# GpSimd's low-part subtractions cut into pieces of at most 256 columns, and one weight-rounding step moved from VectorE to ScalarE

## The chip, the cores and the metric

One core of a Trainium2 chip runs the program. The metric is the device time of one execution in microseconds, the median of several runs. The engines are TensorE (PE in the profile, with PEld its weight loads), VectorE (DVE), ScalarE (ACT), GpSimd (POOL) and SyncE (SP), which issues the DMAs here.

## The reference

Two batches of 3008 x 256 values go through a two-dimensional Fourier transform whose real part is kept, then through two MLPs in sequence over all 6016 tokens.

```
X = np.fft.fft(x, axis=1); X = np.fft.fft(X, axis=2); y = X.real
h = y @ w_in;   r = np.maximum(h, 0.0);  y = (r * r) @ w_out        # 256 -> 2048 -> 256
h = y @ w_in2;  g = h / (1 + np.exp(-1.702 * h));  out = g @ w_out2  # 256 -> 2048 -> 256
```

The weights arrive as float64.

## The kernel before

Matmuls run on operands that are each split in two: a high part, which is the value rounded to the matmul's format by ScalarE (tiles gh, and the first half of w, w2i, eo, ya, yb, yc), and a low part, which is the value minus the high part (tile gl, and the second half of the others). Three products (high x high, high x low, low x high) stand for one. The helper `sub` (L74, L75 in the profile) makes every low part; its first argument says whether VectorE or GpSimd does it, and tables (`LOW`, `LOWE`, `VSTEPS`) choose.

The program has a start (Fourier transform of the first batch), a long first stage, and a second stage. The first stage is a loop of 128 steps over (token block, slice of 128 hidden units). In a step TensorE makes one slice of hidden values in PSUM (`front1`, tile psa, L429 to L431, two psa buffers), VectorE takes it out of PSUM in three operations (p L686, h L688, h L689), ScalarE applies Relu, Square and the rounding (L695, L696, L698; in some steps VectorE does the first two in one operation, L693), and GpSimd in most steps subtracts (gl L75). Four steps later TensorE multiplies gh and gl by the second weights into psb (`back`, L444). A step's `front1` can only start when VectorE has emptied the psa buffer of two steps before.

Beside the steps, jobs run in the background by a table of starts, rates and due steps (`PLAN`): the Fourier transform of the second batch (`fold`, L260 to L278, `even_k`, `odd_k`), and the conversion of the float64 weights (`widen` and `widen_in`, which begin with `narrow`). `narrow` turns the two 32-bit words of each float64 into a float32: absolute value of the high word (ScalarE, L157), clamp (VectorE, L158), shift and mask (VectorE, L159), scaling of the low word by 2^-29 (L163 on ScalarE or L165 on VectorE), then two or three VectorE operations that merge them (L166, L168). The order of instructions on each engine within the first stage is set by a scheduler; each engine then runs its own list in that order, waiting on semaphores. GpSimd's list in the first stage is mainly `sub` in 128 x 752 pieces (two halves of 376 columns), besides folds (L260), sums (L188, L221, L581, L591) and `sub` of weights (128 x 1024, 128 x 512 and 128 x 384).

The second stage (from about 525 us) is written in a fixed order by hand. There `sub` is on VectorE alone, and GpSimd only does sums (L581, L591).

## Time and profile before

| | |
|---|---|
| median of 3 runs | 1037.11 us (1035.15 to 1038.47) |
| the profiled execution | 1035.54 us, of which the span from first to last instruction is 1033.8 us |
| PE busy | 971.6 us (94%) |
| DVE busy | 817.1 us (79%) |
| ACT busy | 616.4 us (60%) |
| POOL busy | 351.4 us (34%) |
[...]

The busy shares are means over stages with different limits. A time in the profile counts from the first instruction; an instruction's duration runs from its start to its end as recorded, and so contains any time that it stood still after it had started. The idle time of an engine and what ended it stand in the chain of waits.

### The profile page before, as it was taken

The numbers are of one execution on the slowest core, as the hardware profiler recorded it, in microseconds if no ns is written. First come the engines' busy times: TensorE is split into PE (matmuls) and PEld (weight loads), VectorE is DVE, ScalarE is ACT, GpSimd is POOL, SyncE is SP. The second block draws the span as 40 slices with busy tenths as digits, with TensorE's granted clock in tenths as the row PEclk, the third lists the DMA queues.
The fourth block names the chain that finished last, engine by engine and source line by source line (L and its number), as shares of the span: only waits on it lengthen the run. The fifth ranks groups of instructions, "written<-read, shape, count | busy, mean of one in ns | idle before, by whom it ended". The sixth has DMA issues, their size and how long they took to land.

```text
span 1033.8 us, 14043 instructions
## 1 busy us (share of the span) xinstructions
PE 971.6 (94%) x5496; PEld 939.3 (91%) x5496; DVE 817.1 (79%) x1088; ACT 616.4 (60%) x764; POOL 351.4 (34%) x216
## 2 busy tenths in 40 slices
PE   4879997899989999999989999999999999999998
PEld 4569887899989889898989999999999999999997
DVE  7995889886777579777658888887988888888875
ACT  2667576775788578797754554554555445454443
POOL 2546464444567446786815210102020020200000
PEclk9999999999999999999999999999999999999999
DMA  7531112101132112101342101000100001000000
GB/s 289 204 127 61 71 71 82 71 31 53 42 129 96 72 55 99 71 31 60 120 132 93 60 31 31 30 31 5 57 1 31 30 26 35 1 31 1 30 1 30
DMA packets 22914, 65.22 MB, mean 63 GB/s; under 512 B 1856, under 2 KB 14272, under 8 KB 19648
## 3 DMA queue, kind: packets, MB, share of 16 engines
q1 hardware_dynamic: 22848, 64.32, 17.4%
q8 instruction: 43, 0.70, 0.3%
q14 instruction: 23, 0.19, 0.1%
HBM read 43.13 MB, written 21.19 MB: 62 GB/s over the span
## 4 chain that ended last, share of the span: by engine, by line
PE 47%; DVE 5%; ACT 4%; issue 1%; POOL 1%; DMA 0%; DVEq 0%; POOLq 0%; ACTq 0%
PE psb L753 24%; PE psa L737 22%; ACT h L696 1%; ACT h L695 1%; DVE gl L75 1%; PE psb L444 1%; ACT gh L698 1%; POOL gl L75 1%; DVE g L789 0%; DVE ue L168 0%; DVE h L689 0%; DMA ydram<-o 0%; DVE p L686 0%; POOL raw L581 0%; DVE h L688 0%
## 5 line engine op out<-in xcount | busy, mean ns | idle before, releaser
L75 POOL TENSOR_TENSOR gl<-h,gh 128x752 fp32r<-128x752 f32 (+1 forms) x113 | 216.0, 1920 | 166.6 <-ACT gh L698 142.1
L444 PE MATMUL psb<-gh,w 128*128 128x376 f32 (+1 forms) x1024 | 240.6, 340 | 4.4 <-ACT o L557 3.5
L753 PE MATMUL psb<-gh,w 128*128 128x376 f32 (+1 forms) x1024 | 237.7, 334 | 0.0
L444 PEld LDWEIGHTS psb<-gh,w 128*128 128x128 f32 x1024 | 185.6, 192 | 6.8 <-ACT o L557 4.7
L753 PEld LDWEIGHTS psb<-gh,w 128*128 128x128 f32 x1024 | 182.9, 188 | 0.0
L695 ACT ACTIVATE h<-h 128x752 f32<-128x752 f32 (+1 forms) x116 | 96.5, 833 | 81.7 <-DVE h L689 77.8
L444 PE MATMUL psb<-gl,w 128*128 128x376 f32 (+1 forms) x512 | 133.7, 341 | 3.2 <-POOL gl L75 2.8
L818 ACT ACTIVATE g<-c 128x1128 f32<-128x1128 f32 (+1 forms) x64 | 73.7, 1152 | 100.1 <-DVE c L816 100.1
L753 PE MATMUL psb<-gl,w 128*128 128x376 f32 (+1 forms) x512 | 129.9, 335 | 0.4 <-DVE gl L75 0.3
L686 DVE SCALAR_TENSOR_TENSOR p<-n,w1n_t,psa 128x376 f32<-128x376 f32 (+1 forms) x128 | 76.5, 601 | 59.7 <-PE psa L431 59.5
L698 ACT CAST gh<-h 128x752 fp32r<-128x752 f32 (+1 forms) x128 | 105.0, 822 | 21.5 <-DVE h L693 14.0
L75 DVE TENSOR_TENSOR gl<-g,gh 128x1504 fp32r<-128x1504 f32 (+1 forms) x64 | 112.2, 1753 | 1.6 <-ACT gh L798 1.6
L429 PE MATMUL psa<-eo,w 128*128 128x376 f32 (+1 forms) x256 | 89.9, 351 | 24.6 <-DVE h L689 19.9
L798 ACT CAST gh<-g 128x1504 fp32r<-128x1504 f32 (+1 forms) x64 | 93.1, 1454 | 32.2 <-DVE g L789 32.2
L591 POOL TENSOR_TENSOR ue<-raw 128x376 f32<-128x376 f32 (+1 forms) x16 | 19.6, 1243 | 271.0 <-DVE ya L75 270.8
L444 PEld LDWEIGHTS psb<-gl,w 128*128 128x128 f32 x512 | 94.6, 193 | 4.8 <-POOL gl L75 4.0
L696 ACT ACTIVATE h<-h 128x752 f32<-128x752 f32 (+1 forms) x116 | 96.6, 834 | 3.2
L753 PEld LDWEIGHTS psb<-gl,w 128*128 128x128 f32 x512 | 92.2, 188 | 1.0 <-DVE gl L75 1.0
L789 DVE TENSOR_TENSOR g<-g,c 128x1128 f32<-128x1128 f32 (+1 forms) x64 | 89.6, 1401 | 1.2 <-ACT g L818 1.2
L815 DVE TENSOR_TENSOR g<-g,psa 128x376 f32<-128x376 f32 (+1 forms) x64 | 35.0, 547 | 68.5 <-ACT g L814 68.5
L430 PE MATMUL psa<-eo,w 128*128 128x376 f32 (+1 forms) x256 | 86.4, 338 | 0.7 <-DVE eo L75 0.7
L431 PE MATMUL psa<-eo,w 128*128 128x376 f32 (+1 forms) x256 | 86.2, 337 | 0.0
(135 smaller groups left out, 1594.3 us busy)
## 6 DMA issues: line engine op xcount, KB each, us to landing
ydram<-o SPq DMA_DIRECT2D x18, 376.0 KB, 2.9
xt<-in_x SPq DMA_DIRECT2D x5, 1024.0 KB, 7.1
cst<-in_dfts SPq DMA_DIRECT2D x8, 570.0 KB, 5.5
raw<-ydram SPq DMA_DIRECT2D x6, 752.0 KB, 4.5
out<-o SPq DMA_DIRECT2D x11, 376.0 KB, 3.1
raw<-in_w1i SPq DMA_DIRECT2D x4, 1024.0 KB, 5.6
raw<-in_w1o SPq DMA_DIRECT2D x4, 1024.0 KB, 4.9
raw<-in_w2i SPq DMA_DIRECT2D x4, 1024.0 KB, 4.9
```

Of the source, the lines that this page charges most:

```text
L75: eng.tensor_tensor(out=o, in0=a, in1=f32(b), op=ALU.subtract)
L429: T.matmul(o, lhsT=w[:, 0, fs], rhs=t[:, par, 0, 0:wd], start=True, stop=False)
L430: T.matmul(o, lhsT=w[:, 0, fs], rhs=t[:, par, 1, 0:wd], start=False, stop=False)
L431: T.matmul(o, lhsT=w[:, 1, fs], rhs=t[:, par, 0, 0:wd], start=False, stop=True)
L444: T.matmul(acc[j][ec][:, s, 0:wd], lhsT=w[:, hl, e0:e0 + P], rhs=(gh, gl)[gi][:, s, 0:wd], start=(first and hl == 0 and gi == 0), stop=(la ...
L695: A.activation(out=hv, in_=hv, func=AF.Relu)
L696: A.activation(out=hv, in_=hv, func=AF.Square)
L698: last_a = A.copy(gh[:, :, 0:wd], hv)
L737: T.matmul(bank, lhsT=w[:, hl, slot * P:(slot + 1) * P], rhs=t[:, yl, i], start=(first and hl == 0 and yl == 0), stop=(hl == 1), skip_grou ...
L753: T.matmul(o[:, s, 0:wd], lhsT=w[:, hl, e0:e0 + P], rhs=g[:, 2 * i + s, 0:wd], start=(f == 0 and hl == 0 and g is gh), stop=(f == 15 and h ...
L789: V.tensor_tensor(out=g[:, 1:4, 0:pw], in0=g[:, 1:4, 0:pw], in1=c[:, :, 0:pw], op=ALU.mult)
L798: A.copy(gh[:, :, 0:pw], g[:, :, 0:pw])
```

## The change

Two things. `sub` on GpSimd is now issued in pieces: a new generator `pieces` walks over all dimensions but the first and the last and cuts the last into equal parts of at most 256 columns. VectorE's subtractions stay whole. And `narrow` always scales the low word on ScalarE: the set `RA`, which named the eight weight groups for which ScalarE did it, and the parameter `key` are gone.

```diff
-RA = {(0, 0, 0), (0, 0, 1), (0, 0, 2), (0, 0, 3), (0, 1, 1), (0, 1, 2), (0, 1, 3), (1, 0, 1)}
...
+    def pieces(*aps):
+
+        if len(aps[0].shape) > 2:
+            for i in range(aps[0].shape[1]):
+                yield from pieces(*(ap[:, i] for ap in aps))
+        else:
+            w = aps[0].shape[1]
+            k = -(-w // 256)
+            for i in range(k):
+                yield tuple(ap[:, i * w // k:(i + 1) * w // k] for ap in aps)
+
     def sub(eng, o, a, b):
-        eng.tensor_tensor(out=o, in0=a, in1=f32(b), op=ALU.subtract)
+        for o, a, b in pieces(o, a, b) if eng is G else ((o, a, b),):
+            eng.tensor_tensor(out=o, in0=a, in1=f32(b), op=ALU.subtract)
...
-    def narrow(raw, ue, key=None):
+    def narrow(raw, ue):
...
-        if key in RA:
-            yield lambda: A.activation(out=eu, in_=lw, func=AF.Copy, scale=2.0 ** -29)
-        else:
-            yield lambda: V.tensor_scalar(out=eu, in0=lw, scalar1=2.0 ** -29, scalar2=None, op0=ALU.mult)
+        yield lambda: A.activation(out=eu, in_=lw, func=AF.Copy, scale=2.0 ** -29)
```

On GpSimd's list, at the conversion of a pair of second-stage weight groups (tile w2i, with the low parts gl of the steps around it), before:

```order
L75 TENSOR_TENSOR gl<-h,gh 128x2x376 x3
L75 TENSOR_TENSOR w2i<-ue,w2i 128x512
L75 TENSOR_TENSOR w2i<-ue,w2i 128x384
L75 TENSOR_TENSOR gl<-h,gh 128x2x376
L75 TENSOR_TENSOR w2i<-ue,w2i 128x512
L75 TENSOR_TENSOR w2i<-ue,w2i 128x384
L75 TENSOR_TENSOR gl<-h,gh 128x2x376 x4
L75 TENSOR_TENSOR w<-ue,w 128x1024
```

The same place of the changed kernel (`sub` is now L86):

```order
L86 TENSOR_TENSOR gl<-h,gh 128x188 x12
L86 TENSOR_TENSOR w2i<-ue,w2i 128x128 x7
L86 TENSOR_TENSOR gl<-h,gh 128x188 x4
L86 TENSOR_TENSOR w2i<-ue,w2i 128x128 x7
L86 TENSOR_TENSOR gl<-h,gh 128x188 x16
L86 TENSOR_TENSOR w<-ue,w 128x256 x4
```

A gl is four instructions in place of one, a w four in place of one, and a half of w2i seven in place of two; their order among each other is the same here.

On VectorE's list, at the conversion of the last weight group of the first stage (tiles raw and ue; p and h belong to the steps), before:

```order
L165 TENSOR_SCALAR ue<-raw 128x1024
L158 TENSOR_SCALAR ue<-ue 128x1024
L686 SCALAR_TENSOR_TENSOR p<-n,w1n_t,psa 128x376
L159 TENSOR_SCALAR ue<-ue 128x1024
L688 TENSOR_TENSOR h<-p,psa 128x376
L689 TENSOR_TENSOR h<-p,psa 128x376
L166 SCALAR_TENSOR_TENSOR ue<-raw,ue 128x1024
```

The same place of the changed kernel (L169 was L158, L170 was L159, L174 was L166, L694 to L697 were L686 to L689):

```order
L169 TENSOR_SCALAR ue<-ue 128x1024
L694 SCALAR_TENSOR_TENSOR p<-n,w1n_t,psa 128x376
L170 TENSOR_SCALAR ue<-ue 128x1024
L696 TENSOR_TENSOR h<-p,psa 128x376
L697 TENSOR_TENSOR h<-p,psa 128x376
L174 SCALAR_TENSOR_TENSOR ue<-raw,ue 128x1024
```

Only the first row is gone; the rest keeps its order. On ScalarE's list at the same conversion, before (L157 is the absolute value, L695, L696 and L698 belong to the steps):

```order
L698 CAST gh<-h 128x2x376
L157 ACTIVATE ue<-raw 128x1024
L695 ACTIVATE h<-h 128x2x376
L696 ACTIVATE h<-h 128x2x376
L698 CAST gh<-h 128x2x376
```

And in the changed kernel (L168 was L157, L173 is the scaling of the low word, L703, L704 and L706 were L695, L696 and L698):

```order
L168 ACTIVATE ue<-raw 128x1024
L703 ACTIVATE h<-h 128x2x376
L704 ACTIVATE h<-h 128x2x376
L706 CAST gh<-h 128x2x376
L173 ACTIVATE ue<-raw 128x1024
```

The scaling now stands on ScalarE one step behind the absolute value. TensorE's list is the same in both kernels.

## Rows read from the trace of the kernel before

**Rows 1.** Busy time of each engine (instructions) in four stretches, us.
```profile
0.00:80.00 80.00, 55.09 (x290) 43.95 (x291) 68.64 (x102) 39.93 (x54) 33.43 (x25) 0.96 0.54 201
...
80.00:220.00 140.00, 125.56 (x692) 120.03 (x691) 114.13 (x163) 94.76 (x118) 75.34 (x40) 0.98 0.20 71
...
400.00:525.00 125.00, 113.87 (x638) 110.53 (x636) 89.94 (x133) 100.44 (x129) 92.26 (x58) 0.98 0.23 81
525.00:1034.00 509.00, 503.49 (x2902) 500.14 (x2901) 412.52 (x490) 252.65 (x301) 53.07 (x31) 1.00 0.09 32
```

**Rows 2.** Waits of TensorE's weight loads, 0 to 80 us: total, times, longest.
```profile
PEld psb L444 <- POOL gl L75: 2.0, 2, 1.8
```

**Rows 3.** The same view, 80 to 220 us.
```profile
PEld psa L429 <- DVE h L689: 13.7, 9, 2.5
```

**Rows 4.** The same view, 220 to 400 us.
```profile
PEld psa L429 <- DVE h L689: 5.4, 5, 3.5
```

**Rows 5.** The same view, 400 to 525 us.
```profile
PEld psa L429 <- DVE h L689: 6.1, 6, 2.1
...
PEld psb L444 <- POOL gl L75: 1.4, 1, 1.4
```

**Rows 6.** Timeline of POOL from 117 us: start, duration, instruction.
```profile
118.50 4.57 POOL L75 TENSOR_TENSOR gl<-h,gh 128x752 fp32r<-128x752 f32 x2 [6.93 <-DVE h L693]
```

**Rows 7.** Timeline of DVE from 117 us.
```profile
119.44 1.96 DVE L166 SCALAR_TENSOR_TENSOR ue<-raw,ue 128x1024 uint32<-128x1024 uint32 x1 [0.21 <-ACT ue L163]
121.33 0.60 DVE L686 SCALAR_TENSOR_TENSOR p<-n,w1n_t,psa 128x376 f32<-128x376 f32 x1
121.84 2.31 DVE L168 CUSTOM_DVE_ANT_0 ue<-ue 128x2048 uint16<-128x2048 uint16 x1
```

**Rows 8.** DVE by shape, 0 to 80 us: count, total us, mean ns, idle before.
```profile
L166 DVE SCALAR_TENSOR_TENSOR ue<-raw,ue 128x1024 uint32<-128x1024 uint32 x5 | 9.9, 1987 | 0.0
L158 DVE TENSOR_SCALAR ue<-ue 128x1024 f32<-128x1024 f32 x6 | 7.3, 1219 | 0.0
L168 DVE CUSTOM_DVE_ANT_0 ue<-ue 128x2048 uint16<-128x2048 uint16 x5 | 6.1, 1217 | 0.0
...
L271 DVE TENSOR_TENSOR xt<-xt 128x512 f32<-128x512 f32 x3 | 2.1, 690 | 0.1
...
L165 DVE TENSOR_SCALAR ue<-raw 128x1024 uint32<-128x1024 uint32 x1 | 0.7, 690 | 0.0
```

**Rows 9.** The same view, 80 to 220 us.
```profile
L276 DVE TENSOR_TENSOR xt<-xt 128x512 f32<-128x512 f32 x2 | 3.9, 1931 | 0.0
L158 DVE TENSOR_SCALAR ue<-ue 128x1024 f32<-128x1024 f32 x2 | 3.7, 1844 | 0.0
L265 DVE TENSOR_TENSOR xt<-t 128x512 f32<-128x512 f32 x2 | 3.5, 1746 | 0.0
```

**Rows 10.** The same view, 220 to 400 us.
```profile
L165 DVE TENSOR_SCALAR ue<-raw 128x1024 uint32<-128x1024 uint32 x5 | 8.0, 1605 | 0.0
L168 DVE CUSTOM_DVE_ANT_0 ue<-ue 128x2048 uint16<-128x2048 uint16 x4 | 7.2, 1798 | 0.0
```

**Rows 11.** The same view, 400 to 525 us.
```profile
L166 DVE SCALAR_TENSOR_TENSOR ue<-raw,ue 128x1024 uint32<-128x1024 uint32 x4 | 6.4, 1606 | 1.2 <-ACT ue L163 1.2
...
L165 DVE TENSOR_SCALAR ue<-raw 128x1024 uint32<-128x1024 uint32 x2 | 4.5, 2274 | 3.0 <-POOL w2i L75 3.0
```

**Rows 12.** Timeline of POOL from 276 us.
```profile
276.85 0.75 POOL L221 TENSOR_TENSOR ue<-ue 128x256 f32<-128x256 f32 x1 [1.23 <-DVE ue L168]
277.56 1.81 POOL L75 TENSOR_TENSOR gl<-h,gh 128x752 fp32r<-128x752 f32 x1
279.32 2.39 POOL L221 TENSOR_TENSOR ue<-ue 128x256 f32<-128x256 f32 x3
```

**Rows 13.** POOL by shape, 400 to 525 us.
```profile
L75 POOL TENSOR_TENSOR gl<-h,gh 128x752 fp32r<-128x752 f32 x35 | 66.2, 1903 | 30.0 <-ACT gh L698 19.0 <-issue 8.3 <-DVE p L686 1.6
```

**Rows 14.** ACT by shape, whole run.
```profile
L163 ACT ACTIVATE ue<-raw 128x1024 uint32<-128x1024 uint32 x8 | 9.1, 1142 | 0.0
```

## The prediction

> **What bounds the kernel now.** I read the busy times by stretch first, then who TensorE's weight loads wait for in each, then the durations of VectorE's and GpSimd's instructions by shape, and last the timelines at one wait. From 525 us on TensorE is busy 503.5 of 509 us [rows 1], and no instruction that the change touches runs there, since `sub` is on VectorE alone in that stage. Half of the time can therefore not move. Before that TensorE is busy 55 of 80 us, 125.6 of 140 us, and 113.9 of 125 us [rows 1]. What it waits for there is mostly one thing: `front1` waits for VectorE's h L689 to empty psa, 13.7 us from 80 to 220 us, 5.4 from 220 to 400, 6.1 from 400 to 525 [rows 3 to 5]. VectorE is busy 68.6 of the first 80 us and 114.1 of the next 140 [rows 1].

> Why is VectorE late? Its durations show it. The custom merge L168 takes 1.22 us in the first stretch and 1.80 on average from 220 to 400 us [rows 8, 10]; L158, which has the size of L165 (0.69 us when nothing is in its way), takes 1.22 and 1.84 [rows 8, 9]; L165 itself takes 1.61 and 2.27 later [rows 10, 11]. The timelines show what is in its way. At 118.50 us two gl of 128x752 start back to back on GpSimd and end at 123.07 [rows 6]. VectorE's L166 starts at 119.44 and needs 1.96 us; L168 starts at 121.84 and needs 2.31 us, to 124.15 [rows 7]. With 1.81 us for one gl [rows 12] the first ended near 120.3, and L166 ended 1.1 us later, which is about what it needs alone. So it stood still until the first gl was done, then ran; the second gl stood still meanwhile (the two need 3.6 us by 1.81 each and took 4.57), and L168 then waited until the second gl had ended. The two engines don't share whatever they contend for: one instruction has it to its end, and between two instructions that stand back to back on GpSimd the waiting VectorE instruction gets it. VectorE's L686, which reads PSUM, ran in 0.60 us in between, at 121.33, while the second gl still had most of its work to do [rows 6, 7]: it doesn't contend, and I take the same of L688 and L689, which read PSUM too.

> **Part 1: shorter GpSimd instructions, what VectorE gains.** A blocked VectorE instruction now waits for a piece in place of a whole gl. A gl took about 1.8 us, a piece will take some 0.57 (worked out below), so one meeting costs a third. Where several contending VectorE instructions follow one another, each meets a piece and the wait is not a third but up to the whole. Because the steps' L686, L688 and L689 stand between most of them and pieces pass beneath these, I take a third as left, two thirds as gained. The waits that I can see in the rows, mean less the time alone, times count:

> - 0 to 80 us: L166 5 x (1.99 - 1.2) = 3.9, L158 6 x (1.22 - 0.69) = 3.2 [rows 8]; 1.2 for L166 alone is from L168, which has the same length. Two thirds of 7.1 is 4.7.
> - 80 to 220 us: L276 2 x (1.93 - 0.69), L158 2 x (1.84 - 0.69), L265 2 x (1.75 - 0.69) [rows 9]; 0.69 for 512 columns of two inputs is L271's [rows 8]. That is 2.5 + 2.3 + 2.1 = 6.9. Two thirds is 4.6.
> - 220 to 400 us: L168 4 x (1.80 - 1.22) = 2.3 [rows 10]; two thirds is 1.5.
> - 400 to 525 us: L166 4 x (1.61 - 1.2) = 1.6 [rows 11]; two thirds is 1.1.

> **Part 2: the low words on ScalarE.** VectorE loses L165: 0.7 us in the first stretch, 8.0 in the third, 4.5 in the fourth [rows 8, 10, 11], durations that contain its waits. ScalarE gains eight instructions of 1.14 us [rows 14], 9.1 us. It is busy 100.4 of 125 us in the fourth stretch [rows 1], so they fit, but each delays a gh by up to 1.14 us. What is queued behind is a step's Relu, Square and rounding, and behind those gl and, four steps later, TensorE's `back`. With four steps in hand I count 1 us in all.

> **Part 3: what GpSimd pays.** From the start of the L221 at 276.85 to that of the gl is 0.71 us for 256 columns, and from the gl to the next L221 1.76 us for 752 [rows 12]. That is 2.1 ns a column and 0.16 us for each instruction, so a piece of 188 columns takes 0.16 + 0.40 = 0.56 to 0.57, four of them 2.25 and a gl 0.48 us more. From 400 to 525 us there are 35 gl [rows 13], 17 us more, where GpSimd is busy 92.3 of 125 us [rows 1]: 109, and the weights' pieces add some more. This is near full. The price is paid where TensorE waits for a gl: 2.0 us in two places of the first stretch and 1.4 us in one of the last [rows 2, 5]. In the last, gl stand in a queue, three of them make 1.4 us; the other two places make 1 us; for places that come to be such, where the end of gl and its use are close already, 1.5 us. Sum 4 us.

> [...]

> **The sum.** What VectorE gains reaches TensorE only where TensorE waits for it. Stretch by stretch: 0 to 80 us, 4.7 + 0.7 = 5.4 gained on VectorE, which is busy nearly throughout, but TensorE and ScalarE have their own turns in the start: I take 3. 80 to 220 us, 4.6 gained against 13.7 waited: 5, a little more than all of it, since other contending forms of that stretch are not in my list. 220 to 400 us, 8.0 + 1.5 against 5.4 waited: 4. 400 to 525 us, 4.5 + 1.1 against 6.1 waited: 4. That is 16, less 4 for GpSimd and 1 for ScalarE. So 11 us off the profiled execution of 1035.5 us gives 1024.5. The median of the runs, 1037.1, is 1.6 us above the profiled execution, so **1026 us**.

> Bounds: if all that TensorE waits behind VectorE goes, 13.7 + 5.4 + 6.1 and 5.4 in the start, and GpSimd costs nothing, 30.6 us go: 1006.5 for the median. If VectorE gains nothing from the pieces, see the second rival.

> **Rivals.** *More of it reaches TensorE*: the gain on VectorE exceeds what I counted, because forms that I left out wait as well and each wait delays all steps behind it. With 25 to 30 of the 30.6 us of the bound gone and 5 paid as above, 20 to 25 us: 1012 to 1017. For it: VectorE is freed of 9.5 and 5.6 us in the third and fourth stretch, about what TensorE waits there. Against: when VectorE is earlier, TensorE runs into ScalarE, which is busy 80% in the fourth stretch, or GpSimd.

> *The lock stays with GpSimd between pieces, and the kernel is slower.* If the pieces of one gl follow so closely that VectorE doesn't get in between, it waits for 2.25 us where it waited for 1.78. The waits counted above, 7.1 + 6.9 + 2.3 + 1.6 = 17.9, grow by 27%, 5 us; GpSimd's price of 4 doubles, as its gl are held by the same VectorE instructions and last longer; moving L165 alone gives back 4 to 8, the gain counted for the third and fourth stretch or half of it. With 1037.1 + 5 + 8 and less 4 to 8 the median is 1042 to 1046. It decides as soon as VectorE fails to get in at more than about half of the pieces' ends. Against it stands the wait shown above [rows 6, 7]: between two gl that stood back to back VectorE did get in. [...] No run here shows yet what happens between pieces that short.

> *GpSimd becomes the bound of the last stretch.* 109 us and the weights' pieces, and at each piece a chance to be held by VectorE for up to 1.2 us. If the fourth stretch takes 125 us as before or 3 us more, its gain of 4 is lost and up to 3 more: of the 11 us 4 to 7 remain, 1030 to 1033, and up to 1037 if the third stretch loses its 4 as well. For it: TensorE waits for a gl there already [rows 5]. Against: 16 us of room.

> **Chances.** My forecast (1018 to 1030) 0.50; more reaches TensorE (below 1018) 0.17; GpSimd bounds the fourth stretch (1030 to 1037) or the gain is hidden otherwise (to 1040) 0.20; the lock stays, or another loss (above 1040) 0.13. 0.3% is 3.1 us, about what can be told from no change here. Faster than 1034: 0.50 + 0.17 + half of the third, 0.76. Same 0.11, slower 0.13. The range that holds 8 in 10 is 1012 to 1038; the likeliest case alone has 1018 to 1030.

> **What would show it.** Step 1: L168 on VectorE near 1.3 to 1.4 us in every stretch, L158 and L159 near 0.8. If they stay at 1.5 and above, pieces don't let VectorE in. Step 2: no scaling of low words on VectorE, 17 on ScalarE (the small w1n included) and no new waits for gh. Step 3: pieces of 188 columns start 0.56 us apart when nothing interrupts; GpSimd's busy time in the fourth stretch rises by 17 us or more; TensorE's waits for gl, now 2.0 and 1.4 us, rise by 5 us at most. The second stage must begin some 11 us before 525 us and take as long as before; if it took longer, the whole argument would miss something. The prediction is wrong if TensorE's waits for h don't fall below 15 us in all, or if they do and waits for gl or ScalarE take their place.

## The result and the profile after

The changed kernel takes 1045.9 us, the median of 5 runs (1043.56 to 1047.14), against 1037.11 before: 1.0086 times, 95% interval 1.0075 to 1.0097. It is slower, by 8.8 us, where 11 us less were forecast. One of the runs of the kernel before that were made beside it took 5343 us, which doesn't move the median. The profiled execution took 1047.14 us, its span is 1045.4 us.

First the first view of before again, busy time of each engine by stretch (TensorE, its weight loads, VectorE, ScalarE, GpSimd, then granted TensorE clock as a share of full speed, DMA share, GB/s), now of after:

```profile
0.00:80.00 80.00, 56.23 (x286) 44.47 (x286) 63.59 (x98) 39.36 (x53) 40.56 (x50) 0.91 0.53 201
80.00:220.00 140.00, 128.09 (x725) 123.97 (x725) 113.38 (x171) 99.41 (x124) 107.98 (x149) 0.99 0.21 72
...
400.00:536.00 136.00, 114.87 (x629) 111.47 (x627) 86.72 (x126) 99.61 (x128) 114.75 (x190) 0.95 0.21 74
536.00:1045.00 509.00, 503.91 (x2903) 500.61 (x2902) 412.83 (x491) 253.12 (x301) 53.16 (x31) 1.00 0.09 32
```

The second stage begins at 536 us where it began at 525 [rows 1], and takes 509 us as before. All is decided in the first stage. From 80 to 220 us TensorE is busier than before (128.1 for 125.6 us); the last stretch takes 136 us for 125, and GpSimd is busy 114.8 us in it for 92.3. Over the whole run TensorE is busy 975.0 us for 971.6 and idle 70.4 for 62.2 (the spans less the busy times): of the 11.6 us by which the span grew, 8.2 are idle time, and 3.4 the same matmuls running longer. The granted clock goes with that: 0.91 for 0.96 in the first stretch and 0.95 for 0.98 in the last. The windows around two long waits of TensorE, same columns:

```profile
418.00:425.00 7.00, 0.89 (x6) 0.58 (x4) 1.00 (x2) 1.22 (x2) 7.00 (x16) 0.72 0.00 0
425.00:429.00 4.00, 3.37 (x11) 3.37 (x12) 4.00 (x6) 3.94 (x6) 1.82 (x4) 0.50 0.52 193
429.00:433.00 4.00, 4.00 (x19) 4.00 (x18) 3.33 (x5) 3.90 (x6) 3.74 (x5) 0.70 0.36 104
...
479.00:483.00 4.00, 3.56 (x12) 3.57 (x13) 3.90 (x7) 3.25 (x4) 0.00 (x0) 0.57 0.00 0
```

From 418 to 425 us TensorE was busy 0.89 of 7 us; from 425 to 429 the granted clock was 0.50, and behind the second wait, from 479 to 483 us, 0.57. Two weight loads took 0.64 us behind each wait (at 427.99 and 481.17 us), for 0.36 ahead of the first (at 416.16). So these two long waits were paid for twice.

Which waits, tells the view of what TensorE's weight loads wait for, the whole run of after: total, times, longest.

```profile
PEld psa L437 <- DVE h L697: 18.1, 9, 5.4
PEld psb L452 <- POOL gl L86: 15.0, 15, 2.0
PEld psb L452 <- ACT o L565: 9.3, 3, 7.0
```

Before, the same view had:

```profile
PEld psa L429 <- DVE h L689: 26.2, 22, 3.5
...
PEld psb L444 <- ACT o L557: 4.7, 4, 2.3
PEld psb L444 <- POOL gl L75: 4.0, 4, 1.8
```

So TensorE waits 8 us less for VectorE, 11 us more for GpSimd's gl, and 4.6 more for ScalarE's o (the store copy that empties psb). By stretch, from 80 to 220 us:

```profile
PEld psb L452 <- POOL gl L86: 5.5, 6, 2.0
PEld psa L437 <- DVE h L697: 5.3, 3, 1.8
```

The wait for h there fell from 13.7 us [rows 3] to 5.3, more than was forecast. From 400 to 540 us:

```profile
PEld psa L437 <- DVE h L697: 9.3, 4, 5.4
PEld psb L452 <- ACT o L565: 7.0, 1, 7.0
...
PEld psb L452 <- POOL gl L86: 3.6, 4, 1.5
```

Here the wait for h rose, from 6.1 us [rows 5] to 9.3, with one of 5.4 in it. The timelines show where that one comes from. VectorE, then TensorE's weight load that follows it:

```profile
471.44 5.92 DVE L169 TENSOR_SCALAR ue<-ue 128x1024 f32<-128x1024 f32 x1 [4.74 <-ACT ue L168]
477.27 0.59 DVE L694 SCALAR_TENSOR_TENSOR p<-n,w1n_t,psa 128x376 f32<-128x376 f32 x1
477.79 0.68 DVE L170 TENSOR_SCALAR ue<-ue 128x1024 uint32<-128x1024 uint32 x1
```

```profile
479.43 0.29 PEld L437 LDWEIGHTS psa<-eo,w 128*128 128x128 f32 x1 [5.43 <-DVE h L697]
```

And GpSimd, start, duration, instruction, number of instructions in the group:

```profile
455.48 6.67 POOL L86 TENSOR_TENSOR gl<-h,gh 128x188 fp32r<-128x188 f32 x12
462.10 2.98 POOL L86 TENSOR_TENSOR w2i<-ue,w2i 128x128 fp32r<-128x128 f32 x7
465.04 2.27 POOL L86 TENSOR_TENSOR gl<-h,gh 128x188 fp32r<-128x188 f32 x4
467.26 2.98 POOL L86 TENSOR_TENSOR w2i<-ue,w2i 128x128 fp32r<-128x128 f32 x7
470.18 6.62 POOL L86 TENSOR_TENSOR gl<-h,gh 128x188 fp32r<-128x188 f32 x12
```

L169 needs 0.68 us when nothing is in its way. It started at 471.44 and stood still until the last group of gl ended at 476.80: ten pieces ended while it waited, and only behind the last, where the row ended, did it get in. The step's L694, queued behind it on VectorE, came 5 us late, and with it the psa buffer for which TensorE then waited 5.43 us. At 512.21 us a second one, yb (128 x 378, 0.54 us alone), took 6.48 us (TensorE then waits 2.74); at 339.69 a third, L701, took 6.21, behind which TensorE had slack. Before, in the same place, the whole forms stood:

```profile
452.84 5.39 POOL L75 TENSOR_TENSOR gl<-h,gh 128x752 fp32r<-128x752 f32 x3
458.17 2.29 POOL L75 TENSOR_TENSOR w2i<-ue,w2i 128x512 fp32r<-128x512 f32 x2
460.40 1.83 POOL L75 TENSOR_TENSOR gl<-h,gh 128x752 fp32r<-128x752 f32 x1
462.18 2.28 POOL L75 TENSOR_TENSOR w2i<-ue,w2i 128x512 fp32r<-128x512 f32 x2
464.41 4.08 POOL L75 TENSOR_TENSOR gl<-h,gh 128x752 fp32r<-128x752 f32 x2
```

```profile
464.50 2.30 DVE L165 TENSOR_SCALAR ue<-raw 128x1024 uint32<-128x1024 uint32 x1 [0.48 <-POOL w2i L75]
```

There VectorE's L165 started at 464.50, took 2.30 us and was let in behind the first of the two gl, although GpSimd had worked without a pause for 12 us. In that row it arrived in the tenth instruction; in after's row L169 arrived in the 34th (both counts begin with one sum, L221 or L229, that runs without a pause ahead of the lines shown).

### The profile page after: what moved, and what is told of

Its sections match the earlier page's. It is cut to its first block, busy times and chain, and to the rows that moved or that the text cites. A ratio compares the mean times of both kernels' runs of the same rounds, so it can differ in the third digit from the quotient of the medians.

```text
span 1045.4 us, 14449 instructions
## 1 busy us (share of the span) xinstructions
PE 975.0 (93%) x5496; PEld 943.6 (90%) x5496; DVE 800.6 (77%) x1079; ACT 624.0 (60%) x773; POOL 446.6 (43%) x628
## 4 chain that ended last, share of the span: by engine, by line
PE 47%; DVE 4%; POOL 3%; ACT 2%; issue 1%; DMA 0%; DVEq 0%; POOLq 0%; ACTq 0%
PE psb L761 24%; PE psa L745 22%; POOL gl L86 2%; DVE ue L169 1%; PE psb L452 1%; DVE yb L86 1%; DVE gl L86 1%; ACT h L704 1%; ACT h L703 1%; POOL w2i L86 0%; DMA ydram<-o 0%; ACT gh L706 0%; POOL raw L589 0%; DVE h L697 0%; DVE h L696 0%
## 5 line engine op out<-in xcount | busy, mean ns | idle before, releaser
L86 POOL TENSOR_TENSOR gl<-h,gh 128x188 fp32r<-128x188 f32 (+1 forms) x452 | 296.9, 693 | 101.9 <-ACT gh L706 75.8
L452 PE MATMUL psb<-gl,w 128*128 128x376 f32 (+1 forms) x512 | 136.7, 344 | 10.7 <-POOL gl L86 10.7
L703 ACT ACTIVATE h<-h 128x752 f32<-128x752 f32 (+1 forms) x116 | 96.2, 832 | 67.1 <-DVE h L697 54.1
L694 DVE SCALAR_TENSOR_TENSOR p<-n,w1n_t,psa 128x376 f32<-128x376 f32 (+1 forms) x128 | 76.7, 601 | 70.1 <-PE psa L439 69.9
L761 PE MATMUL psb<-gl,w 128*128 128x376 f32 (+1 forms) x512 | 129.9, 335 | 0.4 <-DVE gl L86 0.3
L706 ACT CAST gh<-h 128x752 fp32r<-128x752 f32 (+1 forms) x128 | 104.9, 822 | 27.9 <-DVE h L701 24.6
L86 DVE TENSOR_TENSOR gl<-g,gh 128x1504 fp32r<-128x1504 f32 (+1 forms) x64 | 112.2, 1753 | 1.6 <-ACT gh L806 1.6
L704 ACT ACTIVATE h<-h 128x752 f32<-128x752 f32 (+1 forms) x116 | 96.3, 834 | 3.2
```

What stands on the lines that cost most here:

```text
L86: eng.tensor_tensor(out=o, in0=a, in1=f32(b), op=ALU.subtract)
L452: T.matmul(acc[j][ec][:, s, 0:wd], lhsT=w[:, hl, e0:e0 + P], rhs=(gh, gl)[gi][:, s, 0:wd], start=(first and hl == 0 and gi == 0), stop=(la ...
L703: A.activation(out=hv, in_=hv, func=AF.Relu)
L704: A.activation(out=hv, in_=hv, func=AF.Square)
L706: last_a = A.copy(gh[:, :, 0:wd], hv)
L761: T.matmul(o[:, s, 0:wd], lhsT=w[:, hl, e0:e0 + P], rhs=g[:, 2 * i + s, 0:wd], start=(f == 0 and hl == 0 and g is gh), stop=(f == 15 and h ...
```

## The experiments

A row is a run of GpSimd instructions with no idle time between them. Theory A: a long unbroken row of GpSimd instructions keeps a contending VectorE instruction out, and cutting makes rows long; beside that GpSimd is late by its own 0.45 us per gl. Theory B: the scaling moved to ScalarE does the harm. Theory C: only GpSimd's time counts, VectorE is not kept out. All times below are medians of 4 to 10 runs; the kernel before ran beside them with 1036.4 to 1036.8 us, and differences are against that, so that they can be added (the changed kernel: +8.8 against its 1037.1).

**The two parts alone.** In the first, the kernel before gets `pieces` and the new `sub`, nothing else. In the second, the changed kernel gets the old one back:

```diff
...
-        for o, a, b in pieces(o, a, b) if eng is G else ((o, a, b),):
-            eng.tensor_tensor(out=o, in0=a, in1=f32(b), op=ALU.subtract)
+        eng.tensor_tensor(out=o, in0=a, in1=f32(b), op=ALU.subtract)
```

> The kernel before with the pieces alone; the low words are scaled where they were (VectorE for eight groups). Theory A (a long unbroken row of pieces on GpSimd keeps a contending VectorE instruction out, and each gl takes 0.45 us longer): 1041 to 1048 us, and at least two VectorE instructions of 5 us or more that need 0.5 to 1.3 us alone. Theory B (the loss comes from the scaling that ScalarE took over, and the pieces gain): 1026 to 1032 us. Theory C (the pieces cost only GpSimd's 0.45 us per gl, VectorE is not kept out): 1038 to 1043 us with no VectorE instruction kept longer than 3 us.

> The changed kernel with whole subtractions on GpSimd: only the scaling of the low words is moved to ScalarE. A and C (the pieces do the harm): 1030 to 1036 us, since VectorE loses 13 us of work in the last two stretches and ScalarE has room. B (the moved scaling does the harm): 1042 to 1047 us, with a wait of TensorE for ScalarE's o near 425 us of 5 us or more, as in the changed kernel.

Pieces alone: 1045.4 us, +9.0, ratio 1.0078 (1.0051 to 1.0106). Scaling alone: 1031.9 us, -4.5, ratio 0.9961 (0.9948 to 0.9974). So the pieces do the harm, and B falls: the scaling on ScalarE is worth 4.5 us, and on top of it the pieces cost 13.3. With pieces alone TensorE also waits 6.7 us for o near 420 us, so that wait too is the pieces'. One detail of A's expectation missed: there is one VectorE instruction kept over 5 us (7.05 us at 469 us), not two.

**Where.** Only the gl of steps 16 to 75 cut, and the other half:

```diff
-    def sub(eng, o, a, b):
-        for o, a, b in pieces(o, a, b) if eng is G else ((o, a, b),):
+    def sub(eng, o, a, b, cut=False):
+        for o, a, b in pieces(o, a, b) if eng is G and cut else ((o, a, b),):
...
-            sub(G if i not in VSTEPS else V, gl[:, :, 0:pw], h[:, :, 0:pw], gh[:, :, 0:pw])
+            sub(G if i not in VSTEPS else V, gl[:, :, 0:pw], h[:, :, 0:pw], gh[:, :, 0:pw], 16 <= i < 76)
```

> The changed kernel, but only the gl of steps 16 to 75 are cut; the gl of the other steps and all weights are whole on GpSimd. By the shifts of the steps in the two traces the changed kernel gains 7.5 us between steps 15 and 45 and loses it before and behind. A: the gain stays and the later losses go, 1027 to 1033 us, no VectorE instruction kept longer than 3 us behind step 75. B: the losses behind step 75 stay, as the scaling is still on ScalarE, 1039 to 1045 us. C: 1030 to 1036 us.

> The other half of the kernel that cut only the gl of steps 16 to 75: here these are whole, and all other subtractions on GpSimd (gl of steps 0 to 15 and 76 to 127, all weights) are cut. With the scaling on ScalarE and whole pieces throughout 1031.9 us were measured, with the cut of steps 16 to 75 alone 1027.8, with all cut 1045.9. If the parts add up, the cuts outside steps 16 to 75 cost 18 us and this gives 1048 to 1052. If the harm needs the long rows that only appear when everything is cut, 1036 to 1042.

1027.8 us, -8.7, ratio 0.9919 (0.9904 to 0.9934), and 1048.9 us, +12.4, ratio 1.0106 (1.0080 to 1.0131). Against scaling alone the cut of steps 16 to 75 gains 4.2 us, and all the other cuts lose 16.9. Together that is a loss of 12.7, and all cut costs 13.3: the parts add up. The same cut helps in one stretch and hurts in the other.

**Breaking the rows.** In the changed kernel, behind each gl on GpSimd, a copy of its last column, which must wait for the piece before it:

```diff
+    brk = small.tile([P, 1], F32, name="brk")
...
+            if i not in VSTEPS:
+                G.tensor_copy(brk, f32(gl[:, 1, pw - 1:pw]))
```

> The changed kernel with one more GpSimd instruction behind each gl: a copy of the last column of gl, 128 x 1, which has to wait for the last piece and so leaves a gap on GpSimd after every four pieces. Nothing else is changed; GpSimd has more to do. A: no unbroken row of more than four or five pieces is left, the three VectorE instructions that were kept 5 to 6 us are let in after 3 us at most, and of the 10 us that followed them 5 to 10 come back: 1036 to 1041 us, although GpSimd does more. C (only GpSimd's time counts): some 0.25 us more for each gl, 1047 to 1056 us, slower than the changed kernel. B: within 3 us of the changed kernel or slower.

1039.2 us, +2.8, ratio 1.0033 (1.0021 to 1.0045): 6.0 us less than the changed kernel, although GpSimd does more. Its timeline at the same place:

```profile
469.54 2.20 POOL L86 TENSOR_TENSOR gl<-h,gh 128x188 fp32r<-128x188 f32 x4
471.81 0.53 POOL L714 COPY brk<-gl 128x1 f32<-128x1 f32 x1
472.30 3.69 POOL L86 TENSOR_TENSOR gl<-h,gh 128x188 fp32r<-128x188 f32 x4
```

VectorE at that place:

```profile
470.76 1.54 DVE L169 TENSOR_SCALAR ue<-ue 128x1024 f32<-128x1024 f32 x1 [5.58 <-ACT ue L168]
```

The VectorE instruction that took 5.92 us takes 1.54 here; none in the first stage takes over 3 us. C, which expected 1047 to 1056, falls. One detail of A's expectation missed: rows are left of up to 29 instructions, not four or five, because w2i pieces can stand between a gl and its copy, and then the copy has nothing to wait for (at 461.61 and 466.89 us it starts without a pause, where those at 456.39 and 458.84 have 0.06 us ahead of them). L169 arrived in the last instruction but one of such a row; the copy that did wait (at 471.81) ended the row soon, where in the changed kernel nine more pieces followed. GpSimd is now nearly full from 400 to 525 us:

```profile
400.00:525.00 125.00, 109.41 (x610) 106.43 (x609) 73.31 (x122) 96.83 (x125) 120.92 (x219) 0.96 0.20 72
```

**The weights' w2i.** ScalarE's long wait at 424 us, in the changed kernel (its timeline), and GpSimd ahead of it:

```profile
423.78 1.12 ACT L168 ACTIVATE ue<-raw 128x1024 f32<-128x1024 f32 x1 [7.47 <-POOL w2i L86]
424.81 0.77 ACT L565 COPY o<-psb 128x752 f32<-128x752 f32 x1
```

```profile
413.52 3.00 POOL L86 TENSOR_TENSOR w2i<-ue,w2i 128x128 fp32r<-128x128 f32 x7
416.46 4.41 POOL L86 TENSOR_TENSOR gl<-h,gh 128x188 fp32r<-128x188 f32 x8
420.82 2.93 POOL L86 TENSOR_TENSOR w2i<-ue,w2i 128x128 fp32r<-128x128 f32 x7
```

L168 writes the buffer that w2i still reads, and the store copy o, for which TensorE waits 7.04 us, stands behind L168. The two w2i and the two gl between them take 10.2 us; before, they took 8.0 (413.17 to 421.19). The next kernel leaves only w2i whole:

```diff
-    def sub(eng, o, a, b):
-        for o, a, b in pieces(o, a, b) if eng is G else ((o, a, b),):
+    def sub(eng, o, a, b, whole=False):
+        for o, a, b in pieces(o, a, b) if eng is G and not whole else ((o, a, b),):
...
-            yield lambda: [sub(G, l, x, o) for o, l, x in parts]
+            yield lambda: [sub(G, l, x, o, True) for o, l, x in parts]
```

> The changed kernel, but the weights' w2i are whole on GpSimd (4 instructions for a pair in place of 14); gl and w stay cut. In the changed kernel ScalarE waits 7.5 us for the w2i at 424 us and its store copy o stands behind, for which TensorE waits 7.1 us. Theory that the cut of w2i makes that wait: it falls to 4 us or less, and the time by 3 to 5 us, 1041 to 1043. Theory that w2i is late because the cut gl in the same queue are: the wait stays at 5 us or more, and the time is within 2 us of the changed kernel.

1039.6 us, +3.1, ratio 1.0029 (1.0019 to 1.0039): 5.7 us less than the changed kernel, but TensorE's wait for o falls only from 7.0 to 5.6 us. Neither theory had it so: w2i matters as much as the first said, but the wait stays long as the second said, since gl in the same queue are late too. What else went is the third kept instruction (L701, in a row that 14 small w2i had made long) and part of the waits for gl (15.0 to 13.3 us); the other two stay, at 5.92 and 6.49 us. With both repairs:

> The changed kernel with both earlier repairs: the 128 x 1 copy behind each gl, which breaks the rows (alone 1039.2 us), and w2i whole (alone 1039.6). If the two losses are separate, they add up: 1031 to 1035 us. If both repairs mend the same loss (late GpSimd): 1037 to 1040.

1035.2 us, -1.6, ratio 0.9986 (0.9974 to 0.9997): 10.4 us of the 13.3 that the pieces cost are back. The two repairs alone gave 6.0 and 5.7, so the losses are separate but for 1.3 us (the sum expected 1031 to 1035). With both repairs the kernel is still 2.9 us behind scaling alone, each against the kernel before beside it.

**Fewer, longer pieces.** The limit 512 in place of 256 (a gl in two, w2i whole), and the same with four pieces in steps 16 to 75:

```diff
-        if len(aps[0].shape) > 2:
+        if len(aps[0].shape) == 3 and aps[0].shape[2] > 128:
...
+        elif len(aps[0].shape) > 2:
+            yield aps
...
-            k = -(-w // 256)
+            k = -(-w // 512)
```

> The changed kernel with pieces of at most 512 columns in place of 256: a gl is two instructions of 376, a w two of 512, the narrow w2i stay whole. Theory A by count (rows of many instructions keep VectorE out): half as many instructions in a row, so at most one VectorE instruction kept over 3 us, and GpSimd pays 0.16 us more per gl in place of 0.45: 1027 to 1034 us. If any cut below a whole gl is bad: 1038 to 1044 us.

> The kernel with halves, but the gl of steps 16 to 75 in four pieces. If what VectorE gains grows with shorter pieces as long as rows stay short: 1022 to 1025 us, 1 to 4 us below the halves. If the halves already give all that TensorE can use there: 1025 to 1028.

Halves: 1026.0 us, -10.4, ratio 0.9898 (0.9872 to 0.9924), a little below what A gave; but two VectorE instructions of the first stage took over 3 us (3.06 and 3.15) where A had one at most. Quarters, then halves: 1025.3 us, -11.5, ratio 0.9889 (0.9870 to 0.9908), no difference to the halves that these runs can tell. Both beat the kernel before by over 10 us. The waits of TensorE's weight loads in one profiled execution of each say why the second adds nothing (total us, taken from that view):

| kernel | h (VectorE) | gl (GpSimd) | o (ScalarE) | time against before |
|---|---|---|---|---|
| before | 26.2 | 4.0 | 4.7 | 0 |
| changed | 18.1 | 15.0 | 9.3 | +8.8 |
| scaling alone | 18.6 | 4.9 | 7.6 | -4.5 |
| broken rows, w2i whole | 10.9 | 13.0 | 9.3 | -1.6 |
| halves | 16.4 | 5.7 | 7.3 | -10.4 |
| quarters, then halves | 10.8 | 10.9 | 7.0 | -11.5 |

From halves to quarters, then halves, the waits for h fall by 5.6 us and those for gl rise by 5.2. The three columns don't hold the whole gain of the halves: they fall by 5.5 us against before, TensorE's idle time over the span by 7.3 (62.2 to 54.9), and its busy time by 2.4 (971.6 to 969.2).

**The lock by itself.** By lock I mean that one of the two engines keeps the other out. Two kernels, one execution of each, have rows of subtractions on GpSimd and a VectorE clamp (128 x 1024, 0.69 us alone) released in each. In the first:

```python
for i in range(n):
    ...
    G.tensor_tensor(out=o, in0=(r if i == 0 else a)[:, 0:w], in1=f32(b[:, 0:w]), op=ALU.subtract)
    if i == k:
        ...
        V.tensor_scalar(out=r, in0=q[1] if hop else x, scalar1=LEAST, scalar2=TOP, op0=ALU.max, op1=ALU.min)
```

> Computes nothing of the reference: 42 trials, one after the other. In each GpSimd issues an unbroken row of subtractions of SBUF (44 of 188 columns, 30 of 376, 20 of 752, 64 of 94), and one VectorE clamp of 128 x 1024 (the form of L169, 0.69 us alone) is released by the k-th of them, at once, or some 0.3 us later over a small ScalarE copy; k from 2 to 40, the last first piece of each row waits for the clamp of the trial before. Theory A (after a long unbroken row GpSimd's instructions leave VectorE no gap): with 188 columns the clamp takes at most 1.3 us up to some k near 10, and for larger k as long as the rest of the row, 5 to 15 us; if the number of instructions decides, the same count holds with 376, 752 and 94 columns, if time decides, a quarter of it with 752. A rival (VectorE was late for another reason, a semaphore or a buffer, and the row is innocent): one piece's wait for every k, 0.7 to 1.3 us with 188 columns, 1.3 to 2.5 with 752.

Here a clamp either got in behind the next piece or waited to the end of the row, never anything between. Which of the two did not go by k alone, since a row that followed a clamp let in early began without a pause, and so was one row with the rest of the one ahead of it. So the second kernel puts an idle time of 1.5 us or more ahead of each row, over ScalarE:

> Computes nothing of the reference: rows of GpSimd subtractions as in the first such run, but each row begins after an idle time on GpSimd, so that the k-th instruction of the row is the k-th since that idle time. In the first such run the clamp got in after one piece when at most 14 instructions had passed since GpSimd was last idle, at 188, 376 and 752 columns alike, and waited to the end of the row when 18 or more had. Theory (a count of instructions decides): the change falls between 14 and 18 at the same k for 188, 752 and 94 columns, although the rows have then lasted 5, 24 and 8 us. Theory (time decides): it falls at very different k. Then rows with two clamps, the first at the 10th instruction: if the count begins anew when VectorE has got in, the second gets in up to some 15 instructions later and not beyond; if not, it is kept out from the 18th on. Rows with a 128 x 1 copy at the 10th instruction that waits for the piece before it: if that gap is enough to begin the count anew, a clamp at the 19th and 23rd gets in; the same copy of other data, which waits for nothing: no change, the clamp at the 19th is kept out.

VectorE in its timeline, with the clamp released by the 14th and by the 15th instruction of a row, at 188, 752 and 94 columns:

```profile
87.03 1.05 DVE L119 TENSOR_SCALAR r<-q 128x1024 f32<-128x1024 f32 x1 [23.09 <-POOL q L113]
111.17 13.96 DVE L119 TENSOR_SCALAR r<-q 128x1024 f32<-128x1024 f32 x1 [23.08 <-POOL q L113]
...
314.91 2.24 DVE L119 TENSOR_SCALAR r<-q 128x1024 f32<-128x1024 f32 x1 [48.60 <-POOL q L113]
364.02 19.48 DVE L119 TENSOR_SCALAR r<-q 128x1024 f32<-128x1024 f32 x1 [46.88 <-POOL q L113]
...
577.66 0.85 DVE L119 TENSOR_SCALAR r<-q 128x1024 f32<-128x1024 f32 x1 [6.36 <-POOL q L113]
593.61 9.02 DVE L119 TENSOR_SCALAR r<-q 128x1024 f32<-128x1024 f32 x1 [15.10 <-POOL q L113]
```

And GpSimd's row around the second of these:

```profile
103.03 0.58 POOL L113 TENSOR_TENSOR gl<-y,b 128x188 fp32r<-128x188 f32 x1 [1.60 <-ACT y L121]
103.56 7.03 POOL L113 TENSOR_TENSOR gl<-a,b 128x188 fp32r<-128x188 f32 x13
110.55 0.58 POOL L113 TENSOR_TENSOR q<-a,b 128x188 fp32r<-128x188 f32 x1
111.09 12.95 POOL L113 TENSOR_TENSOR gl<-a,b 128x188 fp32r<-128x188 f32 x24
124.00 0.58 POOL L113 TENSOR_TENSOR z<-a,b 128x188 fp32r<-128x188 f32 x1
```

Released by the 14th, the clamp arrives in the 15th and gets in at its end. Released by the 15th, it arrives in the 16th and waits until the whole row has ended, at 124.58. The edge lies at the same instruction for 188, 752 and 94 columns, although the rows had then lasted 8, 26 and 5 us: it is a count. The last trials vary what stands ahead of the clamp:

```profile
750.82 1.05 DVE L119 TENSOR_SCALAR r<-q 128x1024 f32<-128x1024 f32 x1 [6.38 <-POOL q L113]
777.02 7.51 DVE L119 TENSOR_SCALAR r<-q 128x1024 f32<-128x1024 f32 x1 [8.54 <-POOL q L113]
...
846.17 1.05 DVE L119 TENSOR_SCALAR r<-q 128x1024 f32<-128x1024 f32 x1 [24.94 <-POOL q L113]
872.16 7.51 DVE L119 TENSOR_SCALAR r<-q 128x1024 f32<-128x1024 f32 x1 [24.94 <-POOL q L113]
...
940.51 9.66 DVE L119 TENSOR_SCALAR r<-q 128x1024 f32<-128x1024 f32 x1 [13.84 <-POOL q L113]
```

With two clamps, the first released by the 10th instruction and let in, the second gets in when released by the 23rd (1.05 us) and not by the 27th (7.51): the count begins anew. With a 128 x 1 copy behind the 10th that waits for the piece before it (a gap of 0.06 us), a clamp released by the 23rd gets in (1.05 us) and by the 27th doesn't (7.51); with the same copy of other data, which waits for nothing, the one released by the 23rd doesn't (9.66 us).

## Why the prediction was wrong

Two steps failed; mending them gave back 6.0 and 5.7 us of the 13.3 that the pieces cost.

**The first step that failed** is the one that carried all of part 1: "between two instructions that stand back to back on GpSimd the waiting VectorE instruction gets it". It was read from a row of two gl [rows 6, 7] and taken to hold for rows of any length. The trace of before could not show otherwise: in its longest unbroken row VectorE was let in behind the tenth instruction, and a whole gl, w and w2i keep rows that short. Cut into four, four and seven pieces, the same subtractions made eight rows of 16 to 43 instructions, and every contending VectorE instruction that came in the 14th of a row or later waited to the row's end, three of them for 5 to 6 us and three for one more instruction, since the row ended there; none that came earlier did. Rows are counted from the last pause, or the last GpSimd instruction stretched by VectorE, that the records show. By this count two of the long ones came in the 14th and 15th, where an isolated row would still have let them in, and in the kernel with halves yb (at 492.59 us, 3.15 us for 0.55 alone) was kept from the 9th instruction behind a recorded pause of 0.08 us on. So in the real kernel not every recorded pause begins the count anew, or something else keeps VectorE out too; which one is open. Breaking the rows gave 6.0 us back.

**Part 1 otherwise** was right where rows stayed short. From 80 to 220 us the wait for h fell by 8.4 us where 5 were counted, from 220 to 400 by 2.6 (5.4 [rows 4] to 2.8) where 4 were, the moved scaling included. Of the durations named as a sign, the merge L176 is at 1.38, 1.35, 1.45 and 1.41 us in the four stretches, close to the forecast; L169 is at 0.74 in the first but at 1.79 in the second, and at 3.00 in the last, with the kept one in it. One term of the list was only half a gl: of the two L276 (L284 now), one waited behind a gl (at 176.53 us) and one behind a fold (at 205.87), which stays whole; now both meet the fold, and the mean went from 1.93 [rows 9] to 2.47 us.

**Part 2** held in its direction. Alone it gives 4.5 us; 8, less 1 for ScalarE, were in the sum for the third and fourth stretch, pieces included.

**The second step that failed** is the price in part 3, whose unit was right. A gl without interruption takes 2.27 us, the 2.25 of the prediction, for 1.8 whole; TensorE's waits for gl rose by 11 us and not by 4. Even with the rows broken and w2i whole they are 8.1 us above those of scaling alone, while the waits for h are 7.7 below: the cut of gl into four pieces then gains nothing, where the prediction had it gain more than it costs. The three places seen in before were taken for nearly all; but 15 places wait where 4 did. The reading that fits is that a gl stands in a queue behind other gl, so that each 0.45 us adds to the next; no run separates this from the rest. The w2i stood in the prediction only as "the weights' pieces add some more": 14 instructions in place of 4 made 1.4 us a pair (2.98 us for 2.28, twice), where the reuse of a buffer, ScalarE's L168 and behind it the store copy o hang on them. Left whole they gave back 5.7 us, about as much as the broken rows, though part of that is the kept L701.

**The rivals.** The second one, "the lock stays with GpSimd between pieces", forecast 1042 to 1046 and got the time, for a reason that was half right. It priced 2.25 us for each meeting, at all pieces; in fact nearly every meeting went well and a few cost 5 us or more. In the isolated rows the clamp that arrived in the 15th instruction got in at that one's end (1.05 us with 188 columns), and the one that arrived in the 16th waited for the rest of the row, 13.96 us. The third rival, GpSimd bounding the last stretch, is seen in part: 114.8 of 136 us busy, and its gl and w2i waited for.

**The signs and the range.** Both signs of being wrong came: TensorE's waits for h stayed above 15 us in all (18.1), and waits for gl and for ScalarE took the place of those that fell. The range to 1038 left the result out because all above 1040 had a chance of 0.13. (The chance of being faster than 1034, given as 0.76, adds up to 0.77 from its own terms.)

## What to carry to other kernels

Cutting one engine's instructions shorter to let another in paid here only as long as the rows stayed short: count the instructions between two pauses after the cut, not only the length of one. In this kernel a gl in two pieces with w2i whole gave 5.9 us (-4.5 to -10.4), a gl in four with a half of w2i in seven cost 13.3. And where an engine's queue feeds a deadline or a buffer's reuse, the cost of each instruction, about 0.14 us for a subtraction here, adds up along the queue, as the 1.4 us for a pair of w2i did: cut what meets the other engine, leave whole what only delays.
